# One v projection group per block instead of two in a recurrent attention kernel, with a new set of planning priorities

## Chip, cores and metric

The kernel runs on one core of a Trainium2 chip. The metric is the device time of one execution in microseconds (us): the kernel before takes 2164.64 us, the median of two runs (2158.12 and 2171.15). The profile is of one more execution, of 2167.54 us, whose span from the first to the last instruction is 2165.8 us.

## What is computed

Four layers work on x of 2048 rows by 576 columns, in the order A, B, A, B. Both A layers share one set of weights, and so do both B layers. Each adds its result to x.

```
def _A_ref(x, wqkv, wo):                       # 32 heads of 18, window of 8 rows, 2 apart
    q, k, v = split(x @ wqkv)
    logits = einsum('bhsd,bhswd->bhsw', q, k[row - 2*w]) * scale      # w = 0..7
    return einsum('bhsw,bhswd->bhsd', softmax(logits), v[row - 2*w]) @ wo

def _B_ref(x, mem0, Wq, Wk, Wv, Wo, seg_len=32):   # 32 heads of 128, memory of 8 rows
    mem = mem0
    for s in range(64):
        h = concat(mem, x[32*s : 32*s + 32])       # 40 rows
        q, k, v = h @ Wq, h @ Wk, h @ Wv           # for each head
        o = (softmax(mask(q @ k.T * scale)) @ v) @ Wo
        mem, out[s] = o[:8], o[8:]

x = x + _A_ref(layernorm(x)); x = x + _B_ref(layernorm(x), ...)      # and both once more
```

A B layer is a chain of 64 segments: the memory rows that one segment puts out are the first rows of the next. So the 64 steps of a B layer can't be computed side by side.

## The kernel before

**Steps and lanes.** Two lanes run at once. Lane 0 is the first B layer at segment t, lane 1 the second B layer at segment t - 5 (`DLY = 5`), so that step t of 69 works on 80 columns: 32 rows of lane 0, 8 + 8 memory rows, 32 rows of lane 1. The A layers work on tiles of 64 rows (32 tiles each), one tile per step on the average, and their pieces lie between those of the B steps. All weights of B stay on chip; those of A pass through a ring of three buffers that SyncE's queue fills (`wload`).

**One B step** (`b_step`) is made of these pieces. The names are those used later:

- q and k (`qk`, L833 and L836): eleven groups of up to three heads, 27 matmuls each, full 128x128 array. ScalarE or VectorE copies each group out.
- v (`vpass`, L880): up to three blocks of 32 columns, one for each tile V0, V1, V2 (two new blocks in odd steps, three in even ones). For a block, the hidden rows are the stationary operand, 128x32, and four such matmuls of 512 columns run side by side in four column quarters of the array, in five rounds over the 576 rows. Half r of the heads (16 heads) fills one PSUM bank with 20 matmuls. Each half is copied to V by ScalarE (L275) or VectorE (L277).
- scores (`scores`): two groups, S0 for the first 16 heads and S1 for the others. Two full-size matmuls put in the mask (L912), and 48 (32 with one lane) matmuls in column quarters follow (L916, L922). Then VectorE takes the maximum and subtracts it (L771, L772), ScalarE takes the exponential (L774), VectorE sums and inverts (L781, L782), VectorE or GpSimd multiplies (L282), and VectorE transposes into `pt` (L790). This is done for two parts, `em` and `ex`; the multiply of `ex` is on GpSimd.
- the weighted sum (`pv`, L963): pv0 and pv1, one for each half, 48 (or 32) matmuls in row quarters of the array, into four PSUM banks each. Four copies (`OT`) each bring it to SBUF.
- the output projection (`oproj`, L987): eight parts of 20 matmuls, full array. Parts 0 to 3 read pv0's heads, parts 4 to 7 pv1's.
- memory (`mem_out`, L1006 to L1008): VectorE copies the memory rows into the next step's `hT`. x is added by `x_out`, L1026.

The A tiles add projections (L573, L683), layer norm sums (L473), logits (L622, column quarters), the spreading of weights (L647, row quarters) and transposes (L536). `finish_out` transposes the output (L731).

**What sets the order.** Nothing is ordered by hand. Each piece is recorded as an operation of a plan (`_Plan.op`) with its engine or engines, a planned duration, a priority, the operations it comes after, and the buffers that it takes from a pool (`acq`) or holds (`uses`). `_Plan.run` then plays the kernel in planned time: whenever an engine is free, it takes the ready operation with the smallest priority whose buffers are there, and emits its instructions then. For TensorE it holds to the present mode ("F" full array, "C" column quarters, "R" row quarters) if an operation of that mode is ready within a priority distance `w`; `SWITCH`, 0.1, is what it plans for a change of mode. It also plans for the arrival of TensorE's own instructions (`PAGE`, `AHEAD`, `FETCH`). The priorities are a step's number plus an offset from the table `PR`: `v0`, `v1`, `v2` for the three v blocks, `s0`, `s1` for the scores, `p0`, `p1` for the weighted sums, `o` and `od` for the output parts, and so on. On the chip each engine goes through its own list in that order and waits where data isn't there.

**Buffers that matter.** [...] The v operation of a half takes one bank; pv takes four; a scores group takes two. V0, V1 and V2 have one buffer each, `pt`, `em`, `ex` and `hT` two, `qk` seven.

Of the kernel before, what the change touches and what calls it, by code (L numbers as in the profile page):

```python
# [51 lines left out]
class _Plan:  # L52
# [41 lines left out]
    def run(self, log=None):  # L94
# [51 lines left out]
        while left:  # L146
            moved = True
            while moved:
                moved = False
                for e, heap in ready.items():  # L150
# [5 lines left out]
                    while heap:  # L156
                        it = heapq.heappop(heap)
                        o = it[2]
                        if o.done:
                            continue  # L160
                        if alt is not None and o.prio > alt.prio + PR["w"]:
                            skipped.append(it)
# [69 lines left out]
def _act(n):  # L232
    return 0.22 + 0.00072 * n


def _dve(n):
    return 0.15 + 0.00105 * n


def _evac(n):  # L240
    return (_act(n), _dve(n))


AD_ = ("ACT", "DVE")


class _K:
# [271 lines left out]
    def a_tile(self, layer, j, dep, due, span):  # L519
# [5 lines left out]
        def pr(f):  # L525
            return due - span * (1.0 - f)
        Q = PR["A"]
        if layer == 1:
# [33 lines left out]
        for part in (0, 1, 2):  # L562
            ps = pl.buf("r")
            o = o_n
            for c in range(5):
                if c % 2 == 0:
                    n = 256 if c < 4 else P
                    view, w, ow = self.wload(part * 3 + c // 2, self.A_wqkv, (P, 512), part * D + CB[c], n, pr(Q[1]) - PR["ring"], wgate)
                w0 = c % 2 * CB[1]
# [105 lines left out]
        for mb in range(5):  # L675
            if mb % 2 == 0:
                n = 256 if mb < 4 else P
                view, w, ow = self.wload(9 + mb // 2, self.A_wo, (CB[1], CB[4]), mb * P, n, pr(Q[6]) - PR["ring"], o_l)
            w0 = mb % 2 * P
# [177 lines left out]
    def vpass(self, t, k, prio):  # L857

        nc, pl = self.nc, self.pl
        b, c0 = self.vblocks(t)[k] or (None, None)  # L860
        if c0 is None:
            return
        hT, V = self.hT[t], pl.buf(f"V{b}")
        wv, wvr = self.Wb[2]
        self.V[b] = V
        xin = [*self.x_in[t].values()] if k == 1 else [self.x_in[t][0 if k == 0 else 1]]
        if k == 2 and t % 2 == 0 and self.lanes(t)[0]:
            xin.append(self.x_ahead)
        gate = pl.op("NONE", 0.0, None, prio, xin, acq=[V])
        for r in range(2):  # L870
            ps = pl.buf("r")

            def mm(e, r=r, ps=ps):
                for kc in range(5):
                    for c in range(4):
                        if kc < 4:
                            l, w = hT.t[:, kc, c0:c0 + 32], wv[:, kc, (16 * r + 4 * c) * P:(16 * r + 4 * c + 4) * P]
                        else:
                            l, w = hT.t[:, 4 + r, c0:c0 + 32], wvr[:, 4 * c * P:(4 * c + 4) * P]
                        nc.tensor.matmul(ps.t[c * 32:(c + 1) * 32, :], lhsT=l, rhs=w, start=(kc == 0), stop=(kc == 4))  # L880
            o = pl.op("PE", 1.08, mm, prio, [gate] + (self.mem_in[t] if k == 1 else []) +
                      ([self.w_in[2][r], self.vr_in] if t == 0 else []), acq=[ps], uses=[hT, V], mode="C", mm=20)
            self.v_ev[b, r] = pl.op(AD_, _evac(512), lambda e, r=r, ps=ps: self.copy(e, V.t[:, r].rearrange("p i e -> p (i e)"), ps.t[:]),
                                    prio, [o], uses=[ps, V])

    def scores(self, t, r, prio):

# [141 lines left out]
    def b_step(self, t):  # L1029
# [3 lines left out]
        for g in range(11):  # L1033
            self.qk(t, g, t + PR["qk"] + PR["qkd"] * g)
        self.vpass(t, 1, t + PR["v1"])
        self.vpass(t, 0, t + PR["v0"])
# [17 lines left out]
    def trace(self):  # L1054
# [28 lines left out]
        if VERBOSE:  # L1083
# [1 line left out]


DLY = 5
PR = dict(qk=0.388, qkd=0.053, v1=1.358, v0=0.674, w=-0.059, s0=0.001, s1=-1.032, p0=1.109, p1=-0.981, o=0.434,
          od=0.001, mo=0.162, xo=1.055, v2=2.128, a1=2.228, a1s=1.336, a2=0.453, a2s=7.821, fin=5.91, res=-5.123,
          ring=-6.622, A=(-0.03, 0.482, 0.785, 0.737, 0.843, -0.012, 0.929, 0.994))  # L1090
LEAD = 5
COPY = 2
HOLD = False
# [58 lines left out]
```

## Time and profile before

| | |
|---|---|
| time, median of two runs | 2164.64 us |
| span of the profiled execution | 2165.8 us |
| TensorE matmuls | 60,441, 2061.8 us busy |
| VectorE, ScalarE, GpSimd busy | 1392.3, 1169.7, 937.7 us |
| mean granted TensorE clock | 0.992 |
| q and k matmuls (L833, two groups of lines, and L836) | 660.0, 662.5 and 507.2 us busy |
| output projection (L987) | 415.8 us busy |
| v (L880, two groups of lines) | 354.5 and 133.4 us busy |
| memory written and read | 118 GB/s over the span |

The page gives for each engine the time in which at least one of its instructions ran, and that as a share of the span. Matmuls overlap: a busy TensorE says that something was in the array, not that it worked at its peak, and the durations of single matmuls (200 ns for one of 80 columns) are several times the distance from one start to the next (36 ns). So the cost of a piece of TensorE work is read from the starts of its first matmul and of the next piece's first matmul. A group's busy time can't be added to that of another for the same reason.

In the list of waits a line says which engine, at which line of the kernel, waited for what; then the total in us, how often, and the longest. "issue" stands where the profile shows nothing that the engine waited for. In a timeline a row is: start, duration, engine, line, operation, tiles, form, how many of it were merged, and in brackets the idle time before it with what ended it.

### The profile page before, as it was taken

The page shows a single profiled execution, that of the slowest core. Times are in us where ns is not written, and L with a number is a line of the kernel's source. Part 1 is how long each engine was busy: PE and PEld are TensorE (multiplying, and loading weights), DVE is VectorE, ACT ScalarE, POOL GpSimd, SP SyncE. Part 2 cuts the span into 40 slices and gives each one's busy share as a digit, 9 for nine tenths or more (in the row PEclk, how much of TensorE's full clock was granted, in tenths as well). Part 3 has the DMA queues.
Part 4 walks back from the last instruction along what each step waited for, and adds up shares of the span by engine and source line. Part 5 has one row for each costly group of instructions (what it writes and reads, how often), then busy time and mean ns, then how long its engine had stood idle before and what let it go on. Part 6 is the DMA issues. An engine that isn't in the chain of part 4 may idle for free.

```text
span 2165.8 us, 132233 instructions
## 1 busy us (share of the span) xinstructions
PE 2061.8 (95%) x60441; PEld 1727.4 (80%) x60441; DVE 1392.3 (64%) x3525; ACT 1169.7 (54%) x2859; POOL 937.7 (43%) x1325
## 2 busy tenths in 40 slices
PE   2698999999999999999999999999999999999997
PEld 2476888888888888888888888888888888888876
DVE  4466766666666666666666666666666666765675
ACT  2244555555556555555555555555555555655543
POOL 3145444454444544445444454444445445442220
PEclk9799999999999999999999999999999999999999
DMA  9654334343344343334333343333344434332110
GB/s 324 184 155 138 119 108 122 120 131 118 120 125 125 115 128 119 122 119 130 120 115 119 121 135 111 123 122 117 115 132 127 121 112 130 118 119 92 59 57 10
DMA packets 158305, 265.11 MB, mean 122 GB/s; under 512 B 23464, under 2 KB 89904, under 8 KB 157616
## 3 DMA queue, kind: packets, MB, share of 16 engines
q1 hardware_dynamic: 152016, 237.38, 35.8%
q0 software_dynamic: 4576, 18.88, 2.5%
q8 instruction: 472, 7.73, 1.5%
q14 instruction: 89, 0.73, 0.1%
q10 hardware_dynamic: 1152, 0.39, 0.1%
HBM read 240.46 MB, written 16.12 MB: 118 GB/s over the span
## 4 chain that ended last, share of the span: by engine, by line
PE 92%; DMA 4%; DVE 1%; issue 1%; ACT 1%; SPq 0%; POOL 0%; ACTq 0%; POOLq 0%
PE r L833 28%; PE r L987 18%; PE r L880 17%; PE r L573 7%; PE r L836 6%; PE r L963 3%; PE r L683 2%; PE r L912 2%; PE r L473 2%; PE r L916 2%; PE r L647 1%; PE r L922 1%; DMA ring<-strip 1%; DMA ring<-in_A_wqkv_dram 1%; PE r L622 1%
## 5 line engine op out<-in xcount | busy, mean ns | idle before, releaser
L833 PE MATMUL r<-hT,wq 128*128 128x80 bf16 (+1 forms) x8832 | 660.0, 198 | 6.9 <-issue 3.0
L833 PE MATMUL r<-hT,wk 128*128 128x80 bf16 (+1 forms) x8832 | 662.5, 199 | 1.6 <-issue 1.5
L833 PEld LDWEIGHTS <-wq 128*128 128x128 bf16 x8832 | 499.9, 98 | 33.6 <-issue 23.7
L836 PE MATMUL r<-hT,wqk_r 128*128 128x160 bf16 (+1 forms) x2208 | 507.2, 230 | 0.2 <-issue 0.2
L275 ACT ACTIVATE qk<-r 128x480 bf16<-128x480 f32 (+3 forms) x659 | 345.7, 529 | 244.6 <-PE r L836 230.8
L833 PEld LDWEIGHTS <-wk 128*128 128x128 bf16 x8832 | 447.5, 99 | 2.2 <-issue 2.2
L987 PE MATMUL r<-OT,wo 128*128 128x80 bf16 (+1 forms) x11040 | 415.8, 200 | 16.7 <-issue 10.8
L987 PEld LDWEIGHTS <-wo 128*128 128x128 bf16 x11040 | 393.9, 99 | 32.6 <-issue 22.5
L880 PE MATMUL r<-wv,hT 128*32 128x512 bf16 x5376 | 354.5, 382 | 0.0
L282 POOL TENSOR_TENSOR big<-qT,kT 128x1024 bf16<-128x1024 bf16 x188 | 314.3, 1691 | 60.4 <-ACT kT L275 51.9
L282 POOL TENSOR_TENSOR ex<-ex,sum 128x384 bf16<-128x384 bf16 x137 | 116.7, 852 | 468.4 <-DVE sum L782 360.7
L282 POOL TENSOR_TENSOR big<-big 128x1280 bf16<-128x1280 bf16 (+1 forms) x61 | 123.0, 2016 | 422.2 <-DVE big L282 403.6
L880 PEld LDWEIGHTS <-hT 128*32 128x32 bf16 x6720 | 166.2, 96 | 127.1 <-issue 2.6
L275 ACT ACTIVATE V<-r 128x512 bf16<-128x512 f32 x301 | 179.6, 597 | 157.8 <-PE r L880 154.9
L771 DVE TENSOR_REDUCE nmx<-r 128x4 f32<-128x320 f32 (+1 forms) x276 | 143.2, 519 | 163.7 <-PE r L916 162.6
L836 PEld LDWEIGHTS <-wqk_r 128*128 128x128 bf16 x2208 | 219.7, 99 | 0.3 <-issue 0.3
L573 PE MATMUL r<-xn,ring 128*128 128x64 bf16 x4725 | 185.7, 194 | 23.1 <-DMA ring<-in_A_wqkv_dram 18.7
L573 PEld LDWEIGHTS <-ring 128*128 128x128 bf16 x4725 | 161.5, 98 | 44.4 <-DMA ring<-in_A_wqkv_dram 19.9
L275 ACT ACTIVATE OT<-r 128x320 bf16<-128x320 f32 (+1 forms) x375 | 137.5, 425 | 103.8 <-PE r L963 103.3
L275 ACT ACTIVATE big<-r 128x384 bf16<-128x384 f32 (+1 forms) x289 | 110.4, 443 | 88.8 <-issue 65.6
L772 DVE TENSOR_TENSOR r<-r,nmx 128x320 f32<-128x320 f32 (+1 forms) x276 | 147.2, 533 | 9.4
L880 PE MATMUL r<-wv_r,hT 128*32 128x512 bf16 x1344 | 133.4, 380 | 0.0
(150 smaller groups left out, 2906.3 us busy)
## 6 DMA issues: line engine op xcount, KB each, us to landing
ring<-strip SPq DMA_DIRECT2D x488, 320.0 KB, 3.4
ring<-strip SPq DMA_DIRECT2D x244, 160.0 KB, 3.9
x1T<-x SPq DMA_DIRECT2D x32, 160.0 KB, 4.4
x<-x1T SPq DMA_DIRECT2D x32, 160.0 KB, 4.3
x3T<-x SPq DMA_DIRECT2D x32, 160.0 KB, 4.4
x<-x3T SPq DMA_DIRECT2D x32, 160.0 KB, 4.3
wo<-in_B_Wo_dram POOLq DMA_DIRECT2D x4, 1152.0 KB, 30.6
wq<-in_B_Wq_dram POOLq DMA_DIRECT2D x2, 2048.0 KB, 20.6
```

The source lines that it names most:

```text
L275: nc.scalar.activation(out=out, in_=in_, func=ACT.Copy, scale=1.0 if scale is None else scale)
L282: (self.nc.vector if e == "DVE" else self.nc.gpsimd).tensor_tensor(out=out, in0=in0, in1=in1, op=op)
L473: nc.tensor.matmul(psf, lhsT=(self.ones if c < 4 else self.ones_h)[:, :], rhs=xs.t[:, c].rearrange("p a t -> p (a t)"), start=(c == 0), st ...
L573: nc.tensor.matmul(ps.t[:, c * T:(c + 1) * T], lhsT=view()[:, kc, w0:w0 + P], rhs=xn.t[:, kc, :], start=(kc == 0), stop=(kc == 4))
L683: nc.tensor.matmul(ps.t[:, mb * T:(mb + 1) * T], lhsT=view()[:, c, w0:w0 + P], rhs=oT.t[:, c, :], start=(c == 0), stop=(c == 4))
L771: nc.vector.tensor_reduce(out=m, in_=v, axis=AX.X, op=ALU.max, negate=True)
L772: nc.vector.tensor_tensor(out=v, in0=v, in1=m.unsqueeze(len(shp) - 1).to_broadcast(shp), op=ALU.add)
L833: nc.tensor.matmul(pv[:, hh, wi, a:b], lhsT=self.Wb[wi][0][:, kc, h * P:(h + 1) * P], rhs=hT.t[:, kc, a:b], start=(hh == 0 and wi == 0 and ...
L836: nc.tensor.matmul(pv[:, hh, :, a:b], lhsT=self.Wb[0][1][:, h * P:(h + 1) * P], rhs=hT.t[:, 4:6, a:b], start=False, stop=(hh == n - 1), sk ...
L880: nc.tensor.matmul(ps.t[c * 32:(c + 1) * 32, :], lhsT=l, rhs=w, start=(kc == 0), stop=(kc == 4))
L963: nc.tensor.matmul(ps[c].t[:, i * n + a - c0:i * n + z - c0], lhsT=V[b].t[q4, r, i, :], rhs=pt.t[q4, i, b, a:z], start=(i == 0 and b == bl ...
L987: nc.tensor.matmul(psY.t[:, mb * W80 + c0:mb * W80 + c1], lhsT=self.wo[:, w0:w0 + P], rhs=self.OT[:, h % 16 // 4 * 8 + h // 16 * 4 + h % 4 ...
```

## The change

The two halves of a v block become one operation: 40 matmuls on two PSUM banks, taken at the same time, in place of two operations of 20 on one bank each. Its planned duration is 2.16 us in place of twice 1.08, and the planner can no longer put other work between the halves, or change the array's mode there. The two copies to V stay; in the plan both now come after the whole group, where each came after its half. In step 0 the group waits for the loads of both halves of Wv. The priorities of the table `PR` were all set anew, so that the planner makes another order of the whole kernel: `w`, the distance within which it holds to a mode, goes from -0.059 to 0.03, `p0` from 1.109 to 1.329, `s1` from -1.032 to -0.848, `o` from 0.434 to -0.069.

It is meant to keep TensorE longer in one mode.

```diff
         gate = pl.op("NONE", 0.0, None, prio, xin, acq=[V])
-        for r in range(2):
-            ps = pl.buf("r")
-
-            def mm(e, r=r, ps=ps):
+        ps = [pl.buf("r") for _ in range(2)]
+
+        def mm(e):
+            for r in range(2):
                 for kc in range(5):
                     for c in range(4):
...
-                        nc.tensor.matmul(ps.t[c * 32:(c + 1) * 32, :], lhsT=l, rhs=w, start=(kc == 0), stop=(kc == 4))
-            o = pl.op("PE", 1.08, mm, prio, [gate] + (self.mem_in[t] if k == 1 else []) +
-                      ([self.w_in[2][r], self.vr_in] if t == 0 else []), acq=[ps], uses=[hT, V], mode="C", mm=20)
-            self.v_ev[b, r] = pl.op(AD_, _evac(512), lambda e, r=r, ps=ps: self.copy(e, V.t[:, r].rearrange("p i e -> p (i e)"), ps.t[:]),
-                                    prio, [o], uses=[ps, V])
+                        nc.tensor.matmul(ps[r].t[c * 32:(c + 1) * 32, :], lhsT=l, rhs=w, start=(kc == 0), stop=(kc == 4))
+        o = pl.op("PE", 2.16, mm, prio, [gate] + (self.mem_in[t] if k == 1 else []) +
+                  ([*self.w_in[2], self.vr_in] if t == 0 else []), acq=ps, uses=[hT, V], mode="C", mm=40)
+        for r in range(2):
+            self.v_ev[b, r] = pl.op(AD_, _evac(512), lambda e, r=r: self.copy(e, V.t[:, r].rearrange("p i e -> p (i e)"), ps[r].t[:]),
+                                    prio, [o], uses=[ps[r], V])
...
-PR = dict(qk=0.388, qkd=0.053, v1=1.358, v0=0.674, w=-0.059, s0=0.001, s1=-1.032, p0=1.109, p1=-0.981, o=0.434,
-          od=0.001, mo=0.162, xo=1.055, v2=2.128, a1=2.228, a1s=1.336, a2=0.453, a2s=7.821, fin=5.91, res=-5.123,
-          ring=-6.622, A=(-0.03, 0.482, 0.785, 0.737, 0.843, -0.012, 0.929, 0.994))
+PR = dict(qk=0.205, qkd=0.042, v1=1.34, v0=0.68, w=0.03, s0=-0.043, s1=-0.848, p0=1.329, p1=-0.853, o=-0.069,
+          od=0.078, mo=-0.308, xo=0.263, v2=2.167, a1=2.091, a1s=1.353, a2=0.893, a2s=4.855, fin=0.509, res=-4.2,
+          ring=-6.248, A=(0.064, 0.49, 0.615, 0.715, 1.052, 0.85, 0.884, 0.719))
```

The names in the kernel after are the same; its lines behind L884 stand one further down (the mask is L913, the weighted sum L964, the output projection L988).

## The prediction

> **What bounds the kernel now.** I read the page first, then busy time by stretch, then TensorE's waits, then the timelines of one step.
>
> ```profile
> span 2165.8 us, 132233 instructions
> ...
> PE 2061.8 (95%) x60441; PEld 1727.4 (80%) x60441; DVE 1392.3 (64%) x3525; ACT 1169.7 (54%) x2859; POOL 937.7 (43%) x1325
> ...
> q8 instruction: 472, 7.73, 1.5%
> ...
> PE 92%; DMA 4%; DVE 1%; issue 1%; ACT 1%; SPq 0%; POOL 0%; ACTq 0%; POOLq 0%
> ```
>
> TensorE is busy for 95% of the span and is 92% of the chain that ended last. Queue q8 brings TensorE's program: 472 packets, 7.73 MB, for 120,882 loads and matmuls: 256 instructions of 64 bytes a packet.
>
> ```profile
> 400.00:800.00 400.00, 397.46 (x11538) 335.12 (x11534) 265.92 (x667) 230.03 (x555) 188.95 (x266) 1.00 0.40 123
> ```
>
> The second number is TensorE: 397.5 of 400 us. The idle time lies in the first 110 us and the last 60, so only a denser middle makes this kernel faster, and every new wait there counts in full.
>
> ```profile
> PE r L987 <- issue: 10.8, 19, 1.3
> PE r L963 <- DVE pt L790: 6.9, 6, 2.6
> PE r L963 <- issue: 5.2, 12, 1.0
> ...
> PE r L987 <- ACT OT L275: 3.5, 8, 0.9
> ```
>
> TensorE's waits (total, times, longest): for results of other engines next to nothing. Its "issue" waits fall in mid-run, once per 256 instructions, always at the same place of the 256: it waits for its own program.
>
> [...]
>
> ```profile
> 1014.55 0.40 PE L880 MATMUL r<-wv_r,hT 128*32 128x512 bf16 x4
> 1014.77 1.05 PE L880 MATMUL r<-wv,hT 128*32 128x512 bf16 x16
> ...
> 1016.71 0.40 PE L880 MATMUL r<-wv_r,hT 128*32 128x512 bf16 x4
> 1017.04 0.54 PE L963 MATMUL r<-pt,V 32*128 32x48 bf16 x48
> ```
>
> Four v matmuls, then another v half: 0.22 us from start to start. The same four, then a weighted sum (L963) in another mode: 0.33. Over the middle of the trace every kind of mode change costs 0.092 to 0.106 us; I take 0.098. [...]
>
> **The change, part by part.** I compared the built orders of instructions; counts are from there, durations from the trace.
>
> *Arithmetic:* the same 60,441 matmuls. Nothing saved.
>
> *Mode changes:* before, a v half mostly stood alone (237 runs of 20 matmuls, 35 longer); after there are 166 runs of 40 and one of 80. Changes of mode fall from 1150 to 921, counting that the mask matmuls inside a scores group are full-size. 229 x 0.098 = **-22.4 us**, all on the path.
>
> *New order (from the new `PR`):* here lies the price. In the middle the order repeats every two steps. Before, after the second scores group (S1) of a step come some 7 us of other TensorE work until its weighted sum (pv1), in both kinds of step: v halves, projections, pv0, three output parts. S1's softmax needs:
>
> ```profile
> 1043.98 0.49 DVE L771 TENSOR_REDUCE nmx<-r 128x4 f32<-128x320 f32 x1 [1.95 <-PE r L916]
> ...
> 1046.69 0.49 DVE L282 TENSOR_TENSOR em<-em,sum 128x320 bf16<-128x320 bf16 x1
> 1047.20 0.55 DVE L781 TENSOR_REDUCE sum<-ex 128x8 f32<-128x384 bf16 x1
> 1047.78 0.20 DVE L782 RECIPROCAL sum<-sum 128x8 f32<-128x8 f32 x1
> 1047.90 0.53 DVE L790 STREAM_TRANSPOSE pt<-em 128x384 bf16<-128x384 bf16 x1
> ...
> 1049.00 0.71 DVE L790 STREAM_TRANSPOSE pt<-ex 128x512 bf16<-128x512 bf16 x1
> ```
>
> From the first reduction, which starts as S1 ends, to the end of the second transpose: 1049.71 - 1043.98 = 5.73 us. Hidden before, with 1 us to spare.
>
> Odd steps after: S1, 8 spread matmuls, v group, 25 projections, 12 spreads, pv0, one output part of 20, pv1. With mode changes and the trace's rates: 0.11 + 0.23 + 2.28 + 0.83 + 0.20 + 0.54 + 0.82 = 5.0 us. VectorE's order now has a copy of V (0.69, L277) inside the softmax and a copy into `big` (0.45) between the transposes: 2.71 to the first multiply, + 0.69 copy, + 0.51, + 0.58 to the reciprocal, + 1.21 through GpSimd to the second transpose (start to start, 1017.67 to 1018.88 in an even step; the other transpose and the `big` copy fit inside), + 0.71, + 0.05 hand-over = 6.46. pv1 waits **1.45 us**. Part of it comes sooner: the output part stands right behind pv0 and needs its copies. In the last 60 us of before that pairing stalls 0.52 us each time.
>
> Even steps after: S1, v group, 25 projections, v group, 5 transposes, pv0, pv1: 2.28 + 0.83 + 2.28 + 0.24 + 0.43 = 6.1 us. VectorE must copy the second half of the last v group before the second transpose. That half's last matmuls start at 5.19, its copy 0.44 later (1012.55 to 1012.99 before), takes 0.69, then 0.71 and 0.05: 7.08. pv1 waits **1.0 us**. Queued behind pv1 are the output projection, memory and the next step's q and k.
>
> Steps 5 to 63 are 30 odd and 29 even: 43.5 + 29 = **+72 us**. The start and tail have a few more such spots: +2, an estimate. One wait goes: before, 27 steps put five output transposes (L731) between pv0 and L987, and L987 starts 0.18 late: **-5**.
>
> *Program fetch.* I timed each window from 64 instructions ahead of one fetch place to the next, without stalls, and put before's stalls against it: windows under 3.8 us stall 0.52 on average (eight), 3.8 to 4.2: 0.35 (13), 4.2 to 4.6: 0.26 (23), 4.6 to 5: 0.12 (65), longer ones 0.01; 25 us in all. After, the two pv groups stand close together (96 matmuls in 0.9 us in even steps) and 32 windows are under 3.8, 18 of them under 3.4, where the one stall seen (1.1) points to 1.2: 50 us. But the waits above fall into these very windows. With them none is under 3.8, five are under 4.2, 26 under 4.6, 51 under 5: 17 us, **-8**.
>
> *Edits at nothing:* the first v group now needs both halves of Wv; it starts at 87.6 us, where before already runs 60 v matmuls unheld. Twice the banks at once: VectorE and ScalarE (64%, 54% busy) empty them beside matmuls, apart from the waits counted.
>
> Sum: 2164.6 - 22.4 + 72 + 2 - 5 - 8 = **2203 us**, 1.8% slower.
>
> **Unknown costs.** The wait at pv1 is bounded below by the bare softmax, 5.73: 0.7 in odd steps, and in even ones only the copy of V, 6.4 against 6.1: 0.3. That is 30 us in place of 72; fetch then stays near 25. Above: a step without filler in before's tail loses 1.5 to 2.3 us (0.97 or more at pv1, 0.52 at the output part); 1.7 in each would be 100. I take 72, since the order of VectorE is given.
>
> **Rivals.**
> *A, half the waits:* VectorE gets its copies done early and pv1 waits as at the lower bound: 2165 - 22 + 30 + 2 - 5 = 2170, up to 2190 with fetch stalls in their place. For it: V's copy may find gaps. Against: VectorE runs in order, and its order is known.
> *B, slower by over 2%:* the late pv1 pushes the copies of OT, the memory and the next scores, as in before's tail: 100 in place of 72 and fetch at 20: 2165 - 22 + 100 + 2 - 5 - 5 = 2235, from 2208 on. For it: 1.8% is near the border. Against: behind pv1 there are 3 to 4 us before its own output parts.
> *C, faster:* no waits and no new fetch stalls: 2165 - 27 = 2138. Against: without waits fetch takes 25, which gives 2163. Either of the two eats the gain.
>
> **How the numbers follow.** Forecast (2190 to 2208) 0.42, A 0.24, B 0.32, C 0.02. 2203 is the likeliest. 2168 to 2230 leaves out C, the low end of A and the high end of B. Over 2% faster would be under 2121, beyond even C: 0.01. Over 2% slower is B: 0.32. Within: 0.67.
>
> **What would show it.** Right: TensorE's waits list L964 <- DVE pt L790 with 30 to 70 us in some 60 waits, and L988 <- ACT OT L275 with about 15 to 30 in odd steps; the middle stretches drop from 397 of 400 to about 385. Switches: v groups back to back 0.22, TensorE's busy time about 20 us lower. Fetch: "issue" waits at or below before's. Wrong: pv1 waits under 10 us in all (then A or C), or "issue" waits of 40 us or more.

## The result, and the profile after

The kernel after takes **2236.28 us** (two runs, 2235.26 and 2237.31) where the kernel before takes 2164.64 (2158.12 and 2171.15). The ratio is 1.0326, with a 95% interval of 1.0270 to 1.0382: slower by 3.3%. The forecast, 2203, was 33 us short, and the range ended 6 us below the result.

The page of the kernel after: span, engines, TensorE's program queue, and the chain that ended last, by engine and by line:

```profile
span 2233.6 us, 132046 instructions
...
PE 2055.9 (92%) x60441; PEld 1731.9 (78%) x60441; DVE 1420.4 (64%) x3602; ACT 1145.1 (51%) x2841; POOL 842.9 (38%) x1266
...
q8 instruction: 472, 7.73, 1.4%
...
PE 80%; DMA 10%; DVE 5%; issue 2%; ACT 2%; SPq 1%; POOL 0%; ACTq 0%; POOLq 0%; DVEq 0%
PE r L833 25%; PE r L988 15%; PE r L880 15%; DMA ring<-strip 7%; PE r L836 6%; PE r L573 6%; PE r L683 2%; PE r L913 2%; PE r L473 2%; PE r L917 1%; PE r L964 1%; PE r L923 1%; DMA ring<-in_A_wqkv_dram 1%; DVE pt L790 1%; PE r L647 1%
```

TensorE was 92% of the chain and is 80%. What took its place is VectorE, 5% in place of 1%, and DMA, 10% in place of 4%, of which 7% are loads of the ring of weights. These are the surprise. Both kernels ran at a granted clock of 1.00 in the four middle stretches, so the clock is not what parts them there.

Busy time of TensorE (second number) in the middle of the run:

```profile
400.00:800.00 400.00, 381.25 (x11074) 324.36 (x11070) 254.47 (x646) 213.10 (x522) 159.69 (x243) 1.00 0.39 119
```

381 of 400 us, where before had 397. With the three stretches behind it, up to 2000, TensorE is idle for 71.2 us of 1600; before it was 13.9. So the loss lies in the middle, step for step.

TensorE's waits after (total, times, longest):

```profile
PE r L988 <- ACT OT L275: 32.6, 41, 1.0
PE r L964 <- DVE pt L790: 28.6, 37, 2.5
...
PE r L573 <- DMA ring<-strip: 12.7, 22, 1.5
...
PE r L964 <- ACT kT L275: 8.0, 27, 0.6
...
PE r L731 <- DVE fin L1027: 4.5, 24, 0.4
...
PE r L988 <- issue: 4.0, 10, 0.7
...
PE r L683 <- DMA ring<-strip: 2.0, 6, 0.8
```

The output projection waits for copies of OT, the weighted sums wait for the softmax or for a PSUM bank (kT), the A projections for their ring of weights, and the output transposes for VectorE. Waits for reloads of the ring (L573 and L683) sum to 14.7 us. Before they were one line, and L683 had none:

```profile
PE r L573 <- DMA ring<-strip: 3.7, 6, 1.5
```

**An even step** of the kernel after, TensorE and then VectorE, from the second scores group to the output projection (start, duration, engine, line, what, and in brackets the idle time before):

```profile
1039.27 0.33 PE L917 MATMUL r<-qk 128*32 128x80 bf16 x16
...
1043.88 1.04 PE L880 MATMUL r<-wv,hT 128*32 128x512 bf16 x16
1044.74 0.39 PE L880 MATMUL r<-wv_r,hT 128*32 128x512 bf16 x4
1045.07 0.32 PE L536 MATMUL r<-ident,x 128*128 128x64 bf16 x5
1045.32 0.54 PE L964 MATMUL r<-pt,V 32*128 32x48 bf16 x48
1046.55 0.54 PE L964 MATMUL r<-pt,V 32*128 32x48 bf16 x48 [0.69 <-DVE pt L790]
```

```profile
1039.65 0.49 DVE L771 TENSOR_REDUCE nmx<-r 128x4 f32<-128x320 f32 x1 [0.75 <-PE r L917]
...
1043.91 0.53 DVE L790 STREAM_TRANSPOSE pt<-em 128x384 bf16<-128x384 bf16 x1
1045.19 0.69 DVE L277 CAST V<-r 128x512 bf16<-128x512 f32 x1 [0.75 <-PE r L880]
1045.79 0.70 DVE L790 STREAM_TRANSPOSE pt<-ex 128x512 bf16<-128x512 bf16 x1
```

This is what the prediction described. VectorE stands idle for 0.75 us until the last v half is done, copies it, and only then transposes. It keeps to the order of its list: GpSimd's multiply of `ex` (0.83 us from 1044.14) ended at 1044.97, and the transpose of `ex` still started behind the copy, at 1045.79. The transpose ends at 1046.49 and pv1 starts at 1046.55.

**An odd step** of it, TensorE, then ScalarE:

```profile
1077.53 0.90 PE L573 MATMUL r<-xn,ring 128*128 128x64 bf16 x25
1078.36 0.35 PE L647 MATMUL r<-e,epadT 32*128 32x128 bf16 x12
1078.54 0.19 PE L964 MATMUL r<-pt,V 32*128 32x48 bf16 x3
1079.02 0.52 PE L964 MATMUL r<-pt,V 32*128 32x48 bf16 x45 [0.29 <-ACT kT L275]
1080.49 0.88 PE L988 MATMUL r<-OT,wo 128*128 128x80 bf16 x20 [0.95 <-ACT OT L275]
1081.30 0.54 PE L964 MATMUL r<-pt,V 32*128 32x48 bf16 x48
```

```profile
1078.53 0.44 ACT L275 ACTIVATE kT<-r 128x320 bf16<-128x320 f32 x1 [0.28 <-PE r L573]
1078.86 1.25 ACT L275 ACTIVATE big<-r 128x384 bf16<-128x384 f32 x3
1079.97 1.46 ACT L275 ACTIVATE OT<-r 128x320 bf16<-128x320 f32 x4
```

Here the time is lost ahead of pv1. pv0 has started three matmuls when its fourth PSUM bank (the kernel's pool `r` has eight buffers) is still held by a projection, whose copy (kT) ScalarE makes only now. Then ScalarE copies three pieces of `big` before OT, so that the output part right behind pv0 starts 0.95 late. When pv1's turn comes its `pt` is there.

**Where the 68 us between the two profiles went.** I took TensorE's own pace from the trace of before (for each kind of work the distance from start to start when nothing holds it, and 0.098 us a change of mode), laid the order of each kernel out at that pace, and called every gap above it a loss, by what stands on its two sides. The middle is matmuls 6,000 to 57,000 (276 to 2,051 us before, 279 to 2,116 after); start and tail are the rest.

| us | before | after | difference | in the prediction |
|---|---|---|---|---|
| unstalled work of TensorE | 2057.7 | 2035.2 | -22.5 | -22.4 |
| middle: at the weighted sums, and the output part behind pv0 | 0.7 | 65.6 | +64.9 | +72 |
| middle: at projections whose weights come through the ring | 0.6 | 16.3 | +15.7 | no term |
| middle: at or behind the output transposes (L731) | 4.7 | 7.6 | +2.9 | -5 |
| middle: program fetch | 21.4 | 20.8 | -0.6 | -8 |
| start and tail | 90.0 | 99.4 | +9.4 | +2 |
| rest (the pace is a little too slow for both) | -9.3 | -11.3 | -2.0 | |
| span | 2165.8 | 2233.6 | **+67.8** | +38.6 |

The rows differ a little from one profile to the next: r10 below has nearly the order of after, and r2 a pv wait moved in it; they have 12.7 and 18.1 us at the ring where after has 16.3, and 15.2 and 18.9 of fetch where after has 20.8. So no difference of 5 us in these two rows is read as an effect.

### The profile page after: what moved, and what is told of

The parts are those of the page before. It is cut to its first block, busy times and chain, and to the rows that moved or that the text cites. A ratio compares the mean times of both kernels' runs of the same rounds, so it can differ in the third digit from the quotient of the medians.

```text
span 2233.6 us, 132046 instructions
## 1 busy us (share of the span) xinstructions
PE 2055.9 (92%) x60441; PEld 1731.9 (78%) x60441; DVE 1420.4 (64%) x3602; ACT 1145.1 (51%) x2841; POOL 842.9 (38%) x1266
## 4 chain that ended last, share of the span: by engine, by line
PE 80%; DMA 10%; DVE 5%; issue 2%; ACT 2%; SPq 1%; POOL 0%; ACTq 0%; POOLq 0%; DVEq 0%
PE r L833 25%; PE r L988 15%; PE r L880 15%; DMA ring<-strip 7%; PE r L836 6%; PE r L573 6%; PE r L683 2%; PE r L913 2%; PE r L473 2%; PE r L917 1%; PE r L964 1%; PE r L923 1%; DMA ring<-in_A_wqkv_dram 1%; DVE pt L790 1%; PE r L647 1%
## 5 line engine op out<-in xcount | busy, mean ns | idle before, releaser
L988 PE MATMUL r<-OT,wo 128*128 128x80 bf16 (+1 forms) x11040 | 412.3, 200 | 39.1 <-ACT OT L275 32.6
L275 ACT ACTIVATE qk<-r 128x480 bf16<-128x480 f32 (+3 forms) x569 | 296.3, 533 | 267.0 <-PE r L836 261.2
L988 PEld LDWEIGHTS <-wo 128*128 128x128 bf16 x11040 | 395.8, 100 | 44.5 <-issue 41.4
L573 PE MATMUL r<-xn,ring 128*128 128x64 bf16 x4725 | 189.0, 194 | 38.5 <-DMA ring<-in_A_wqkv_dram 21.1
L573 PEld LDWEIGHTS <-ring 128*128 128x128 bf16 x4725 | 161.5, 98 | 70.7 <-issue 29.6
L277 DVE CAST qk<-r 128x480 bf16<-128x480 f32 (+3 forms) x190 | 115.5, 608 | 134.2 <-PE r L836 117.4
L275 ACT ACTIVATE big<-r 128x384 bf16<-128x384 f32 (+1 forms) x412 | 157.1, 442 | 79.5 <-PE r L647 74.7
L275 ACT ACTIVATE V<-r 128x512 bf16<-128x512 f32 x231 | 137.6, 597 | 99.5 <-PE r L880 95.6
L275 ACT ACTIVATE OT<-r 128x320 bf16<-128x320 f32 (+1 forms) x380 | 135.8, 435 | 55.6 <-PE r L964 54.1
L282 POOL TENSOR_TENSOR xnb<-x,st 128x256 bf16<-128x256 f32 x124 | 64.6, 521 | 257.4 <-DVE st L479 257.4
L275 ACT ACTIVATE xs<-x 128x320 bf16<-128x320 f32 x128 | 59.7, 467 | 186.9 <-DVE x L689 170.1
```

What stands on the lines that cost most here:

```text
L275: nc.scalar.activation(out=out, in_=in_, func=ACT.Copy, scale=1.0 if scale is None else scale)
L277: (nc.vector if e == "DVE" else nc.gpsimd).tensor_copy(out=out, in_=in_)
L282: (self.nc.vector if e == "DVE" else self.nc.gpsimd).tensor_tensor(out=out, in0=in0, in1=in1, op=op)
L573: nc.tensor.matmul(ps.t[:, c * T:(c + 1) * T], lhsT=view()[:, kc, w0:w0 + P], rhs=xn.t[:, kc, :], start=(kc == 0), stop=(kc == 4))
L988: nc.tensor.matmul(psY.t[:, mb * W80 + c0:mb * W80 + c1], lhsT=self.wo[:, w0:w0 + P], rhs=self.OT[:, h % 16 // 4 * 8 + h // 16 * 4 + h % 4 ...
```

## Experiments

Theory, after the result: the saved mode changes are real; the new order pays for them with waits behind the shorter stretch from S1 to pv1; and a denser TensorE then meets the ring loads, which the prediction had left out. Rivals: the late pv1 alone drags the rest with it (rival B); or grouping the halves is itself to blame, whatever the table of priorities.

Most experiments must not let the planner answer an edit with another order. In them the plan is made first and its instructions are emitted afterwards in the plan's order, so that one thing can be changed with everything else in its place:

```diff
-                    if o.fn is not None:
-                        o.fn(e)
+                    emit.append((e, o))
...
+        for e, o in self.edit(emit):
+            if o.fn is not None:
+                o.fn(e)
```

This moves line numbers by some lines: in the lines shown below, pv is L970 or L971 where after has L964, the output projection L994 or L995, the A projections L579; they move further where an edit is longer. Ratios are to the kernel before on the same chip, with their 95% intervals. Losses are counted as in the table above; "pv", "ring" and "fetch" are its second, third and fifth row.

### 1. The softmax taken from pv1 (r1_nosoft), the OT copies from the output part (r2_noot), both (r3_both)

r1: pv1 reads the softmax of the first half of the heads, long done. r2: in steps 6 to 63 the first output part reads what an earlier pv1 left in OT in place of pv0's new rows. Both compute something else at these places; the order of every engine stays.

```diff
+        first = self.PT[0][0]
...
-                        nc.tensor.matmul(ps[c].t[:, i * n + a - c0:i * n + z - c0], lhsT=V[b].t[q4, r, i, :], rhs=pt.t[q4, i, b, a:z],
+                        nc.tensor.matmul(ps[c].t[:, i * n + a - c0:i * n + z - c0], lhsT=V[b].t[q4, r, i, :], rhs=first.t[q4, i, b, a:z],
```

```diff
-                        nc.tensor.matmul(psY.t[:, mb * W80 + c0:mb * W80 + c1], lhsT=self.wo[:, w0:w0 + P], rhs=self.OT[:, h % 16 // 4 * 8 + h // 16 * 4 + h % 4, c0:c1],
+                        nc.tensor.matmul(psY.t[:, mb * W80 + c0:mb * W80 + c1], lhsT=self.wo[:, w0:w0 + P], rhs=self.OT[:, h % 16 // 4 * 8 + (1 if k == 0 and 6 <= t < 64 else h // 16) * 4 + h % 4, c0:c1],
```

> The kernel after, its order of instructions on every engine kept; pv1 reads the softmax of S0 in place of S1's, so that it does not wait for S1's second transpose (left out: the second half of the heads is weighted with the first half's weights; all work on all engines stays). My theory (the new order leaves VectorE too little time between S1 and pv1): in even steps the wait of 0.87 us at pv1 shrinks to the wait for its copy of V, about 0.25; in odd steps nothing changes, since there TensorE waits before the output part that stands ahead of pv1. 29 x 0.6 = -17 us: about 2219, 'L964 <- DVE pt L790' close to 0. Rival (these waits only fill time that would go to program fetch anyway): 2230 or more.

> The kernel after, order kept; in steps 6 to 63 output part 0 reads pv1's slot of OT as the step before left it, so that it does not wait for pv0's copies (left out: heads 0 to 3 of these steps are replaced by stale ones). My theory: in odd steps the wait of 1.03 us ahead of the output part goes, but pv1 right behind it then waits for its second transpose, which ends 6.5 us after S1 against 5.5 for TensorE: the wait only moves. 0 to -5 us: 2231 to 2236, with 'L988 <- ACT OT L275' gone and 'L964 <- DVE pt L790' up by 25 us. Rival (the copies of OT alone are what holds the odd steps): -30, 2206.

> The kernel after, order kept, with both of these edits. My theory: the two waits stand behind each other, so only both together free the odd steps. pv1 then waits there for its PSUM banks alone (copies into big end 5.65 after S1): -0.85 in each odd step, -0.6 in each even one, -42 us, of which program fetch takes back 10 to 20, because the windows with pv0 and pv1 close together run under 3.8 us again: 2204 to 2214, 'issue' waits up from about 20 to 30 to 40 us. Rival without the fetch coming back: 2194. Rival of additive waits: the sum of the two single runs.

| | median us | ratio | pv | ring | fetch | tail |
|---|---|---|---|---|---|---|
| after | 2236.28 | 1.0326 (1.0270 to 1.0382) | 65.6 | 16.3 | 20.8 | 10.6 |
| r1 | 2228.12 | 1.0289 (1.0266 to 1.0312) | 50.0 | 23.6 | 24.2 | 6.5 |
| r2 | 2237.47 | 1.0316 (1.0299 to 1.0333) | 57.4 | 18.1 | 18.9 | 10.6 |
| r3 | 2223.68 | 1.0253 (1.0230 to 1.0276) | 27.2 | 35.9 | 26.9 | 8.3 |

In r1 the wait at pv1 of even steps fell from 0.84 to 0.23 us (what is left is put down to the copy of V), and odd steps kept their 0.45 and 0.99: in odd steps the softmax is not what ends the wait. About 2219 was expected and 2228 came: of the 15.6 us that went at pv, 8 show in the medians, while the ring's row rose by 7.3. The intervals of r1 and after overlap, so on the clock alone r1 shows no gain clear of noise. r2 is the same as after, but the wait has moved (its profile is of a run 7 us under its median). TensorE's waits in r2:

```profile
PE r L970 <- DVE pt L796: 45.8, 63, 2.5
...
PE r L994 <- ACT OT L281: 7.3, 14, 1.0
```

With the OT copies out of the way, odd steps wait for the softmax instead, 0.73 us at pv1. So two waits of nearly the same end stand one behind the other, and removing one brings up the other. r3 takes away both, and 38.4 of the 65.6 us of pv waits go. The span of the profiled run falls by 8.5 only; the median is 13.8 under that of r2 on the same chip, and above the 2204 to 2214 that were expected:

```profile
PE r L579 <- DMA ring<-strip: 24.6, 33, 1.9
...
PE r L995 <- issue: 9.8, 18, 1.6
```

The ring's waits rise by 19.6 us, which was not expected, and program fetch by 6.1, just beyond what two profiles differ by. That is the third layer: TensorE gets to its next weights, and to its next instructions, sooner than these come. This speaks against rival B: if the late pv1 alone were the cause, most of the 38 us would have come off the clock; 13 came by the medians of r3 and after, 16 by the ratios. It is no full test, since 27.2 us of pv waits stay in r3, and no run takes away pv waits and ring loads together.

### 2. The ring loads taken away (r4_noring, and from the kernel before, r8_noring_before)

From their third load into the ring on the weights of A are not fetched; the projections read what lies in the ring, so that their results are others. These loads are 200 of the 265 MB that the DMA queues move in the kernel after (r4's page has 65), not the 35% that the expectation for r4 names. All instructions of the engines but SyncE's stay in their order.

```diff
-        o = pl.op("SP", 0.9 if k <= COPY else 0.5, gather if k <= COPY else fetch, prio, [dep, self.strip_in.get(i)], acq=[w], lat=4.0)
+        o = pl.op("SP", 0.9 if k <= COPY else 0.5, gather if k <= COPY else None, prio, [dep, self.strip_in.get(i)], acq=[w], lat=4.0)
```

> The kernel after, order kept; from the fourth use on the weights of the A layers are not fetched into the ring again (left out: these loads; the A layers use stale weights; the matmuls stay). This takes away the waits of TensorE for ring loads, 14.7 us in the trace, which the prediction did not have, and 35% of the DMA traffic. My theory: these waits are real losses: -13 to -20 us, 2216 to 2223. Rival (a wait for the ring only delays work that would wait at pv1 anyway): -5 or less.

> The control to the run of the kernel after without the ring loads: the kernel before, its order kept, with the same loads left out (the A layers use stale weights; all matmuls stay). In the kernel after this took away 14 us of waits for the ring, 18 us of waits for the program and 9 us at the start. My theory: before hardly waits for the ring (0.6 us in the middle), so here only the waits for the program (21 us in the middle) and the start go: -25 to -30 us, 2137 to 2142, against -42 in the kernel after. Rival (the program's fetch is slow by itself, not by the ring's loads): -5 to -12.

r4: 2194.21 us, ratio 1.0121 (1.0106 to 1.0136), 42 less than after, over twice what was expected: that had only the ring's waits in it, and program fetch and some of the start went too. r8: 2136.21 us, ratio 0.9896 (0.9875 to 0.9918), 24 less than before, about as expected. The losses by the same count:

| | start | pv | ring | fetch | tail |
|---|---|---|---|---|---|
| after | 88.8 | 65.6 | 16.3 | 20.8 | 10.6 |
| r4, after without ring loads | 79.5 | 68.3 | 0.0 | 1.8 | 8.6 |
| before | 84.7 | 0.7 | 0.6 | 21.4 | 5.3 |
| r8, before without ring loads | 76.1 | 0.7 | 0.0 | 0.7 | 3.7 |

The pv waits stay, ring and fetch go. TensorE's waits in r4, then its middle stretch in r8:

```profile
PE r L994 <- ACT OT L281: 33.2, 42, 1.0
PE r L970 <- DVE pt L796: 31.0, 40, 2.5
...
PE r L737 <- DVE fin L1033: 5.2, 28, 0.4
```

```profile
400.00:800.00 400.00, 399.89 (x11654) 338.15 (x11655) 267.61 (x671) 230.99 (x557) 191.16 (x264) 1.00 0.06 17
```

Two things follow. Without ring loads the change costs 1.0121 / 0.9896 = 1.0227, with them 1.0326: by the ratios some 21 us of the 72 hang on the ring loads. The profiles give less: the spans of r4 and r8 are 57.7 us apart where those of after and before are 67.8, which leaves 10. r4 and r8 ran on different chips, so 10 to 21 us is what can be said, and some 50 to 58 hang on the rest. In the middle the rest closes: r4 takes 1805.5 us there and r8 1753.4, 52 more, and its waits are 67.6 longer at pv and some 4 at the output transposes, against some 20 saved in changes of mode. And the waits for the program are all but gone without the ring loads, in both kernels (20.8 to 1.8 us and 21.4 to 0.7). r8 is the kernel before at 399.9 busy of 400 with the DMA engines busy for 0.06 in place of 0.40.

The ring waits could have been counted from the order alone. A load of the ring can start when the last projection on its buffer is done, and takes 3.3 us (the page's median, 320 KB) or 3.7 (160 KB) from issue to landing. Of the 688 reloads of the steady part, laid out at TensorE's unstalled pace, the same buffer is wanted again within 5 us in 35 cases before and in 232 after. One such case, right after the even step shown above, on TensorE and then on SyncE's queue:

```profile
1054.23 0.90 PE L573 MATMUL r<-xn,ring 128*128 128x64 bf16 x25
...
1059.87 0.46 PE L573 MATMUL r<-xn,ring 128*128 128x64 bf16 x10
1061.84 0.47 PE L573 MATMUL r<-xn,ring 128*128 128x64 bf16 x10 [1.51 <-DMA ring<-strip]
```

```profile
1054.72 0.32 SPq L510 DMA_DIRECT2D ring<-strip  x1
1055.14 0.37 SPq L718 DMA_DIRECT2D x<-x1T  x1
1055.61 0.38 SPq L510 DMA_DIRECT2D ring<-strip  x1
1056.04 0.42 SPq L718 DMA_DIRECT2D x<-x3T  x1
1056.56 0.38 SPq L510 DMA_DIRECT2D ring<-strip  x1
```

25 projections in one run use up all three buffers. The three reloads go out one by one with loads of x between them, and the second buffer is wanted 4.7 us after its load was issued and comes after 6.2.

### 3. Which half of the change is it: r6_grp_oldpr and r7_sep_newpr

r6 has the grouped operation with the old table `PR`; r7 has the two separate operations with the new table.

> The grouped v operation with the old table PR; nothing left out. The planner makes a third order from it, with 1095 mode changes. My theory: the table is fitted to one structure, and the planner, which takes any ready operation, leaves TensorE without fillers when one is changed alone: slower than both kernels, about 2280 (the planner's own end is 2251 us, against 2124 for before, which takes 2165, and 2208 for after, which takes 2236). Rival (the new table is what costs, the grouping is good): faster than after, at or below 2165.

> The two separate v operations of before with the new table PR; nothing left out. 1026 mode changes, the planner's own end 2267 us. My theory: about 2295, slower than both kernels, for the same reason. Rival (the grouping costs, the new table is as good as the old): at or below 2175.

r6: 2232.15 us, ratio 1.0328 (1.0297 to 1.0358). r7: 2269.38 us, ratio 1.0510 (1.0481 to 1.0540). Both were expected some 25 to 48 us worse; the signs held. By count r6 saves 5.4 us of mode changes and r7 12.3. In the middle r6 loses most at pv after projections (14.9) and at the output projection after logits (14.7) and after projections (8.9). r7 loses 40.4 us where q and k come right after the output transposes and wait for ScalarE's copies into `hT`; TensorE's waits in r7:

```profile
PE r L833 <- ACT hT L275: 42.9, 30, 2.8
```

So grouping with the old table costs as much as grouping with the new one, in another order. The new table is no improvement that the grouping spoils, and it is useless without the grouping. A table of priorities belongs to the operations for which it was set.

### 4. The halves joined in the order of the kernel before: up (r5_join), down (r9_down), down where it pays (r11_down2)

The kernel before, its order kept, and only the v halves moved: r5 moves the second half up behind the first, in the 95 of 168 blocks where a bank is free for it; r9 moves the first half (and its copy, if that came earlier) down to the second, in 131 of 168 blocks; r11 does as r9 in 65 blocks, only where mode changes fall and where the first half does not stand between q, k and a scores group.

The core of r5:

```diff
+            order.remove(second)
+            order.insert(order.index(first) + 1, second)
```

of r9 and r11 (`out` is the copy of the first half):

```diff
+            order.remove(first)
+            order.insert(order.index(second), first)
+            if not late:
+                order.remove(out)
+                order.insert(order.index(second) + 1, out)
```

and what r11 adds ahead of that:

```diff
+            if runs(pe[a - 1:a] + pe[a + 1:b] + [first] + pe[b:b + 2]) >= was or (pe[a - 1].mm in (18, 27) and pe[a + 1].mm in (34, 50)):
+                continue
```

> The grouping alone: the kernel before, its order of instructions kept but for 95 of the 168 v blocks, whose second half's matmuls are moved up to stand right behind the first half's (in a PSUM bank that is free there). Nothing is left out. Mode changes only fall from 1151 to 1133, because between two v halves before mostly stand scores, which share the v's mode at one side. My theory (the loss comes with the new order, not with the grouping; and the grouping as such saves few mode changes): 18 x 0.098 = -2 us, within 5 us of before. Rival (the grouping itself costs, by late copies to V and two banks at once): +10 us or more, with waits of L963 for V.

> The grouping the other way: the kernel before, its order kept, but in 131 of the 168 v blocks the first half's matmuls are moved down to stand right ahead of the second half's (its copy to V behind it, a free PSUM bank). Nothing is left out. Mode changes fall from 1151 to 966, and the v work between S1 and the weighted sums, which hides S1's softmax, stays there or grows. My theory after the run that joined upward (31 us lost: the scores came 1.08 us later and the filler behind them went): here S1 comes earlier, so no new wait at pv1; 185 x 0.098 = -18 us, less some 5 us of new small waits: 2145 to 2155 against 2162 to 2167 for before, a gain of 0.5 to 0.9%. Rival (grouping itself costs, wherever it stands): slower than before by 10 us or more.

> As the run that joined downward, but only where the mode changes fall by it and where the v half doesn't stand between q and k and the scores that read them: 65 of 168 blocks, 1151 to 1026 mode changes; nothing is left out. In the run with 131 blocks 18 us of mode changes went, and 8 us came back as waits inside the scores for copies of q and k, 11 as waits for ring loads. My theory (a join is worth its mode changes, less the waits that the earlier pieces around it run into): 125 x 0.098 = -12 us, with 1 to 4 us of waits: 0.3 to 0.5% faster than before. Rival (TensorE is held at this pace by the ring loads and the program's fetch whatever it saves): no faster than before.

| | median us | ratio | mode changes | unstalled work | what is lost in the middle |
|---|---|---|---|---|---|
| r5, up | 2191.12 | 1.0148 (1.0126 to 1.0170) | -18 | -1.6 us | 10.7 at sums of the layer norm after q, k; 9.6 within the transposes; pv 8.3 |
| r9, down | 2164.88 | 1.0024 (1.0016 to 1.0032) | -185 | -18.0 us | 8.3 within scores groups, ring 11.2 |
| r11, down, chosen | 2165.54 | 0.9985 (0.9974 to 0.9995) | -125 | -12.2 us | ring 4.2 |

r5 was expected within 5 us of before and is 31 slower. Joining up puts 1.08 us more (20 v matmuls; in the trace of before four start within 25 ns of each other, one in each column quarter, and the next four 0.22 us later) ahead of all that stood between the halves, the scores above all, and takes the filler away behind them; that this is why it loses is argued from where the waits stand. TensorE's waits in r5 (L508 is the layer norm's sums, L766 the output transposes) name copies of ScalarE, whose list kept its order:

```profile
PE r L508 <- ACT xs L502: 17.7, 31, 5.8
...
PE r L766 <- ACT V L309: 5.5, 25, 0.2
```

r9 was expected at 2145 to 2155. It saves the 18.0 us and loses them again: 8.3 at the scores (0.3 us in each even step, where the first half stood between q, k and S0 and hid the copies of q and k), 10.6 at the ring and 6 in start and tail. Fetch is 10.3 lower in its profile; but the profile of before is of a run 7 us above the median that before has on r9's chip, so this difference is not taken for an effect of the join. Of 688 reloads of the ring 91 are wanted within 5 us, and TensorE's waits show it:

```profile
PE r L616 <- DMA ring<-strip: 9.4, 16, 1.8
```

r11 leaves those blocks alone and is the only version here that beats both kernels: 2165.54 against 2169.17 on the same chip, 0.15%. It was expected to give 0.3 to 0.5%. Of its 12.2 us 3.6 show on the clock and 3.6 more are waits for the ring (4.2 where before has 0.6); where the rest went was not traced.

r9 and r11 settle the rival that grouping is itself to blame: in the order of before the halves can be joined in 131 blocks at a cost of 0.2%, with no new waits of that size at pv. Where they are joined, and what then stands between S1 and pv1, decides.

### 5. The join without ring loads (r12_down_noring)

r9 with the edit of r4: from the third load into the ring on, the weights of A are not fetched.

> The run that joined 131 blocks downward, with the ring loads left out as in the two runs above (the A layers use stale weights). Left out of the kernel before, these loads gave -24 us. If what the join saved came back as waits for the ring: -18 from the mode changes, +8 for the scores and +4 at the tail stay, so about 6 to 10 us under the kernel before without ring loads, 0.3 to 0.5%, where with the loads the join was 0.2% slower. Rival (the ring is not what took it back): 0.2% slower here too.

2136.20 us, ratio 0.9845 (0.9828 to 0.9861). Against r8, the kernel before without ring loads, 0.9845 / 0.9896 = 0.9948: by the ratios the join then makes the kernel 0.5% faster, where with ring loads it made it 0.2% slower. The loss at the scores stays (8.1), that at the ring goes (0.2). This fits the ring loads having taken the join's gain back, but does not show it: the two medians themselves are equal (2136.20 and 2136.21), on two chips on which before differs by 0.4%, so the 0.5% rests on the ratio to before. In the profiles the middle is 6.3 us shorter in r12 than in r8 (1747.1 and 1753.4), and what stands ahead of it 5.6 longer.

### 6. The output transposes (r10_fin)

In the kernel after, 24 steps have the five transposes of `fin` right behind 25 projections, and they start 0.3 us late. r10 exchanges VectorE's two additions (L1027) so that `fin` is added before lane 0's x.

```diff
+        at = [i for i, (e, o) in enumerate(emit) if e == "DVE"]
+        for i, j in zip(at, at[1:]):
+            if emit[i][1].tag == 0 and emit[j][1].tag == 1:
+                emit[i], emit[j] = emit[j], emit[i]
```

> The kernel after, order kept but for one exchange: VectorE adds the second lane's rows (fin, which TensorE transposes right after) ahead of the first lane's. Nothing is left out. The trace of the kernel after shows 7.6 us of waits ahead of these transposes (24 of 0.32 us). If they are real losses: -6 to -8 us, 2228 to 2230. Rival (something else waits in their place, such as the layer norm of the first lane): no change.

2228.38 us, ratio 1.0311 (1.0295 to 1.0327): the ratio is that of after, so the time within the range expected is owed to the chip, and the waits are still there (8.2 us). The exchange took place only in odd steps; in the even ones, where the transposes wait, `fin` was first already. So this says nothing on the cause of these 7.6 us, beyond that the order of the two additions isn't it. It stays open.

## Why the prediction was wrong

Point by point, in the order of its sum.

- **Mode changes, -22.4: right.** By count -22.5. The trace shows it directly too: the middle less its losses over 0.08 us took 1747.1 us before and 1725.3 after, 21.8 less, where the count has 19.7 less for that part. From v half to v half 0.22 (1043.66 to 1043.88), as the prediction said a group would show.
- **Waits at pv1, +72: the size right, the place right in even steps alone.** Even steps: 1.0 predicted, 0.84 measured, by the very chain that was named (VectorE waits for the last v half, copies it, transposes). Odd steps: 1.45 predicted at pv1, 1.44 measured in sum, but 0.45 at pv0's fourth bank (the prediction had put the banks at nothing) and 0.99 at the output part behind pv0. The prediction said that "part of it comes sooner"; all of it does. S1's first reduction to the end of the second transpose took 6.08 us there (1074.90 to 1080.98) where 6.46 less the hand-over was worked out. 65 us lie in the middle and some more in the last steps (r1 takes 4.1 off the tail).
- **The sum has no term for the ring: the step that failed.** Its paragraph "Edits at nothing" looked for what else could wait and named Wv and the banks, not the three ring buffers, though the waits of before listed them (3.7 us) and though the order was at hand. Measured: +15.7 in the middle by the count, +11.0 in the two lines of waits for L573 and L683 together, and 10 to 21 us on the clock (r4 against r8). It is the largest single miss, about half of the 33 us; three smaller terms, below, were mis-sized the same way.
- **Program fetch, -8: mis-sized, measured -0.6.** The waits did fall into the densest windows, so that the 50 us of an unheld order did not come; the 17 us expected were 20.8. The windows were right as a description, but not the cause by themselves: r8 shows the same order almost without stalls once the ring loads are gone. The traces tie the waits to the fetch: the 472 packets of q8 have 16,384 bytes each, one for every 256 of the 120,882 loads and matmuls; in before the 29 TensorE waits over 0.2 us between 162 and 2000 us for which the profile names no releaser all end 1.2 to 1.6 us after a packet of q8 has ended, and in after all 17 end 1.2 to 1.8 us after one. Their place among the 256 is not quite the same: it drifts evenly, from 189 to 159 in before and from 187 to 159 in after. That the stalls need the ring loads beside them is shown by r4 (1.8 us left), r8 (0.7) and r12 (4.5 us of "issue" waits in its list, where r9 has 9.5) alone. That the fetch's packets and the loads hinder each other in the DMA engines is the author's argument and was not shown; it rests on one count: from 64 instructions (the planner's `AHEAD`) ahead of a fetch place, nine packets of ten start within some 2.9 us in before and 2.1 in r8, and within some 3.2 in after and 2.3 in r4.
- **The output transposes, -5: the wait named went, another came.** The 4.7 us behind them are gone; ahead of them 7.6 came, because they now follow 25 projections and need an addition of VectorE. Net +2.9.
- **Start and tail, +2: mis-sized, measured +9.4.** 4.1 in the start, 5.3 in the tail. r1 puts most of the tail's part on the softmax. For the start no experiment was made that parts it from the ring loads, which weigh on it in both kernels (84.7 to 76.1 in r8, 88.8 to 79.5 in r4).

The sum of the misses: -7.1 at pv, +15.7, +7.4, +7.9 and +7.4, in all +31.3. With -0.1 for the mode changes and -2.0 for the rest that makes the 29.2 us by which the profiles' difference (67.8) passes the 38.6 of the sum; by the medians it is 33. Four of five point the same way: each of these waits was taken to shrink or to stay as it was.

**Rival B** gave 2235, the number that came, and for a reason that did not. It wanted 100 us of waits at and behind pv1; these were 65.6, and r3 gives 13 us back when 38 of them are removed. That its number came is luck: the ring and the other terms made up for the waits that it had too many of.

**The signs that were named.** L964 <- DVE pt L790 with 28.6 us in 37 waits lies just under the 30 to 70 in 60, since half of the waits stand under OT; L988 <- ACT OT L275 with 32.6 is just over its 15 to 30; the middle stretches have 381 to 384 of 400, 385 was said; TensorE's "issue" waits are not above those of before, as said. TensorE's busy time fell by 5.9 and not by 20: the busy time counts matmuls that overlap (about 200 ns each where the next starts 36 ns later) and was the wrong view for the switches, for which the starts are the right one.

## What to carry to other kernels

Count what a denser order saves, but then go through every resource that the engine waits for in the new order, loads through small rings included: how long after the last use of a buffer is it wanted again, against the load's time to land (here 688 reloads of 3.3 to 3.7 us, 232 of them wanted within 5 in the kernel after). Work that stands between a producer and its consumer is worth the latency that it hides: here the order of after saves 22 us of mode changes and lets 65 us of waits show that the work between S1 and pv1 had hidden before. On TensorE, busy for 381 to 384 of 400 us in the middle of the kernel after, waits stand one behind the other, and the removal of one was worth what the next left, not its own size: r2 took 25.3 us off the waits for OT and nothing off the clock, r3 38.4 us off the waits at pv and 13 to 16 off the clock.

## What was not expected of the hardware

- TensorE's waits for its own program are not a matter of its pace alone. The kernel before loses 21.4 us to them with the ring loads and 0.7 without (r8), at the same instructions in the same order; the kernel after 20.8 and 1.8 (r4).
- In r2 a wait of nearly equal end came in the place of the one removed: it took 25.3 us off the list's waits for OT (32.6 to 7.3), 17.2 us came back as waits for `pt` (28.6 to 45.8), and the time did not change (ratios 1.0316 and 1.0326).
